# Fused attention and feed-forward kernel: the second set-aside score moved up by half a row, and full-height products between two score pairs

## The chip, the cores and the metric

The kernel runs on one core of one Trainium2 chip. Its time is the device time of one execution in microseconds (us), and what is compared is the median over several executions. TensorE multiplies matrices and writes its results to eight banks of accumulators (PSUM); VectorE (DVE), ScalarE (ACT) and GpSimd (POOL) do the rest of the arithmetic, and SyncE (SP) issues most of the transfers. The engines run side by side and wait for each other only through semaphores.

## The reference

All tensors are float32. `x` is 2048 x 512; attention has 32 heads of 16 channels, the feed-forward layer 1792 hidden units.

```python
xn = layernorm(x)
q, k, v = split_heads(xn @ wqkv)               # 32 heads of 16
p = softmax(einsum("bhqd,bhkd->bhqk", q, k) * 16 ** -0.5)
s = merge_heads(einsum("bhqk,bhkd->bhqd", p, v)) @ wo
h = relu(xn @ w1 + b1) ** 2
g = silu(h @ w2 + b2)
out = x + s * g
```

## The kernel before, in words

To keep precision, every large operand is held as two rounded halves, a high part and a low part, and a product is the sum of three: high by high, high by low, low by high.

After a first stage (normalising, transposing, queries, keys, values) comes the main loop, 128 turns of it. A turn handles four steps; one step is one block of 128 keys against 512 queries for four heads. For a step, four scores are computed, one for each head (`score`, L282). Each uses only 64 rows of the array (16 channels, four times over for the parts), so two run at the same time: one on the lower half of the rows (half 0), the other on the upper half (half 1). Such a pair of products I call a row of work. `scores(i, p)` makes a row, a score pair of 128 x 1024 in a buffer `S`, and `exps` (L286, ScalarE) turns it into exponentials straight from there. There are two buffers `S` in the main loop.

One step in four, the last of the turn, is set aside: `aside(i, p, hp)` writes one single score to the one bank `lin` (called `single`), and VectorE copies it to SBUF (L305); when two copies are there, ScalarE takes the exponential from SBUF. A set-aside score fills one half of a row, and there are four of them in a turn. As there is one bank, each must wait until the one before it has been copied.

Between these stands filler: the matrix products of the feed-forward layer and, in the last sixteen turns, of the output projection. They are written as pairs of `Block`s, two results of 128 x 512 in the two banks of `spare`. A block's list `todo` holds its products over 128 rows; `issue` (L330) does one of them on one half of the rows, so that a product needs two issues, one on each half, in any order. `lin(0, 1)` issues one product on each half: a row of filler. `lin(0)` or `lin(1)` alone fills the half beside a set-aside score. In the first part of a pair, half 0 works on block 0 and half 1 on block 1; `swap()` issues what is left and exchanges them; the second `swap()` calls the blocks' `evict`, in which VectorE reads `spare`.

Most pairs of blocks have twelve products each and take two turns, with the swap between the turns. The blocks of `second` with g = 0 have six products each. They start and end in one turn (`make and end` in the loop), with the first swap in the middle of it: the two-pair turns, eight of 128. Every full turn has six score pairs, four set-aside scores and 24 halves of filler: twenty rows. At its end `values` (L538) multiplies the exponentials by the values, 32 products of 128 rows and 32 columns of the array for four steps.

The order of instructions on each engine is the order of the program text; nothing reorders it. The waits follow from the data. The order of TensorE's rows before, in a turn that isn't a two-pair turn: score pair 1; set-aside 1 beside filler; score pair 2; four rows of filler; filler beside set-aside 2; score pair 3; two rows; score pair 4; set-aside 3 beside filler; two rows; score pair 5; two rows; filler beside set-aside 4; score pair 6; values. Score pairs 5 and 6 belong to the next turn's first step. In a two-pair turn before: five rows of filler ahead of set-aside 2; nothing between score pairs 3 and 4, where the swap is; then set-aside 3, one row, score pair 5, four rows, set-aside 4, score pair 6.

Of the kernel before, what the change touches and what calls it, by code (L numbers as in the profile page):

```python
# [73 lines left out]
def fast_path(tc, sb, ps, env):  # L74
# [6 lines left out]
    mm = nc.tensor.matmul  # L81
# [4 lines left out]
    def t(shape, dt, tag):  # L86

        cnt[0] += 1
        p = ps if tag in ("S", "lin", "acc") else sb
        if tag in BUFS:  # L90
            turn[tag] = turn.get(tag, -1) + 1
            n = turn[tag] % BUFS[tag]
            tag = f"{tag}{places[n] if tag == 'S' else n}"
        return p.tile(shape, dt, tag=tag, name=f"{tag}_{cnt[0]}")
# [181 lines left out]
    ptile = {}  # L276

    def score(i, p, hp, dst):
        qd, qc, kb = steps[i]
        k, q = ka[qd, kb // 8], qa[qd, qc]  # L280
        r = slice(64 * hp, 64 * hp + 64)
        mm(dst, k[r, p, 128 * (kb % 8):128 * (kb % 8) + 128], q[r, p], start=True, stop=True)  # L282

    def exps(i, p, src):
        if src is not None:
            act.activation(ptile[i, p], src, AF.Exp, scale=SCALE)  # L286

    def place(i, p):
        ptile[i, p] = t([128, 2, 512], FT, f"P{2 * ((i - 1) % 4) + p}")

    def scores(i, p):

        if i < len(steps):
            sc = t([128, 2, 512], FT, "S")
            place(i, p)
            for hp in range(2):
                score(i, p, hp, sc[:, hp])
            return sc

    def aside(i, p, hp):  # L300

        if hp == 0:
            place(i, p)
        score(i, p, hp, single)
        dve.tensor_copy(ptile[i, p][:, hp], single)  # L305
# [5 lines left out]
    class Block:  # L311


        def __init__(self, lhs, rhs, ks, evict, late=(), upper=()):

            pairs = [(a, b) for a, b in ((0, 0), (0, 1), (1, 0))]
            todo = ([(k, a, b) for a, b in pairs for k in ks if k not in late] +
                    [(k, a, b) for k in late for a, b in pairs])
            self.todo = todo, [d for d in todo if d[0] not in upper]
            self.lhs, self.rhs, self.evict, self.at = lhs, rhs, evict, [0, 0]  # L320

        def issue(self, half, bank):
# [8 lines left out]
               stop=n == len(self.todo[half]) - 1 and self.at[other] > 0)  # L331
            return True

    pair, swapped = [None], [0]

    def lin(*halves):
        if pair[0]:  # L340
            for half in halves:
                j = half ^ swapped[0]
                pair[0][j].issue(half, lin_banks[j])

    def swap():
        if pair[0]:
            while any([pair[0][half ^ swapped[0]].issue(half, lin_banks[half ^ swapped[0]]) for half in range(2)]):
                pass
            swapped[0] ^= 1
            if not swapped[0]:  # L350
                pair[0][0].evict()
                pair[0] = None
# [21 lines left out]
    def split_piece(eng=None):  # L374
        if at_piece[1] == len(pieces):
            return
        j, layer, m = pieces[at_piece[1]]
        at_piece[1] += 1
        raw, q = raws.pop(0), PAIRS[m][1]
        wf[layer, m] = [t([128, 4, 256] if layer == 1 else [128, 2, 512], FR, f"wf{layer}{p}{q}") for p in "hl"]  # L380
        split(*wf[layer, m], raw, eng or dve, pool)
        load_piece()
# [15 lines left out]
    def second(c, g, i):  # L398
        ms = [m for m in range(len(PAIRS)) if PAIRS[m][0] == g]
        h, w = [hid[m] for m in ms], [wf[2, m] for m in ms]  # L400

        def evict():
            if g == 0:
                y[c, i] = t([128, 2, 512], FT, f"y{i}")
            old = b2b.unsqueeze(1).broadcast_to([128, 2, 512]) if g == 0 else y[c, i]
            dve.tensor_tensor(y[c, i], spare, old, op=OP.add)
            if g == 3:
                complete.add((c, i))

        return [Block(lambda p, k, j=j: h[k // 2][p][:, k % 2, 128 * j:128 * j + 128],  # L410
                      lambda p, k: w[k // 2][p][:, k % 2], range(2 * len(ms)), evict)
                for j in (2 * i, 2 * i + 1)]
# [8 lines left out]
    for c in ORDER:  # L421
        for m, (g, _) in enumerate(PAIRS):
            fill += [(lambda m=m: first(m), False), (None, True)]
            if m in (1, 2, 4, 6):
                for i in range(2):
                    make = lambda c=c, g=g if m > 1 else 0, i=i: second(c, g, i)
# [9 lines left out]
    for i in range(4):  # L436
        part = vt[:, 4 * i:4 * i + 4]
# [11 lines left out]
    for n in (0, 0, 1, 1, 0, 1, 2):  # L449
# [15 lines left out]
    todo = [[(k, a, 0) for n in (0, 2) for a in range(2) for k in (n, n + 1)],  # L465
            [(k, a, 0) for a in range(2) for k in range(4)]]
# [65 lines left out]
    def values(i):  # L532
        qd, qc, kb = steps[i]
        if kb == 0:
            acc[0] = t([128, 512], FT, "acc")
        for j in (1, 2, 3, 0) if i % 2 else (0, 1, 2, 3):
            o = (4 * qd + j) * 17
            mm(acc[0][32 * j:32 * j + 32], vt[:, kb, o:o + 32], ptile[i, j // 2][:, j % 2],  # L538
               start=kb == 0, stop=kb == NK - 1)

    def finish(i):

        qd, qc, kb = steps[i]
        if kb < NK - 1:
            return
        if i == len(steps) - 1:
            return
        ou = t([128, 512], FT, "ou")
        cast(act if turn_ends_first[0] else dve, ou, acc[0])
        sp.dma_start(zdram[qd][qc], ou[16::32])  # L550
        for j in range(4):
            sp.dma_start(udram[qd // 2][qc][0, qd % 2, :, j], ou[32 * j:32 * j + 16])
        n = i // 4
        events.setdefault(2 * n + 2, []).insert(0, (load_sums, (qd, qc)))
        at(n + 2, rowsums, qd, qc)
# [174 lines left out]
    def happen(time):  # L730
        for fn, a in events.pop(int(2 * time), ()):
            fn(*a)


    n = turn["S"]
# [3 lines left out]
    lin_banks = [spare[:, 0], spare[:, 1]]  # L739
# [3 lines left out]
    def rest(i, dst):  # L743

        group(dst, lambda p: onorm[2, 3][p][:, cut[i]], lambda p: wos[0][p][:, 3])

    def end_rest(i, src):

        o = t([128, 512], FT, f"wf2{'hl'[i // 2]}{i % 2}")
        dve.scalar_tensor_tensor(o, src, 0.5, gsb[2, i // 2][:, i % 2], op0=OP.mult, op1=OP.mult)  # L750
        pool.dma_start(out[1024 + 128 * i:1152 + 128 * i], o, accum_op=OP.add)

    turn_ends_first = [False]
    for n in range(TURNS):
        i = 4 * n
        happen(n)
        make, end, split_now = fill[n]
        if make:
            pair[0] = make()
        exps(i + 1, 0, scores(i + 1, 0))  # L760
        aside(i + 3, 0, 0)
        lin(1)
        exps(i + 1, 1, scores(i + 1, 1))
        for _ in range(5 if make and end else 4):
            lin(0, 1)
        if make and end:
            lin(0)
            aside(i + 3, 0, 1)
            exps(i + 2, 0, scores(i + 2, 0))
            swap()  # L770
            exps(i + 2, 1, scores(i + 2, 1))
            aside(i + 3, 1, 0)
            lin(1)
            exps(i + 3, 0, ptile[i + 3, 0])
            lin(0, 1)
            last = [scores(i + 4, 0)]
            for _ in range(4):
                lin(0, 1)
        else:
            lin(0)  # L780
            aside(i + 3, 0, 1)
            exps(i + 2, 0, scores(i + 2, 0))
            lin(0, 1)
            lin(0, 1)
            exps(i + 2, 1, scores(i + 2, 1))
            aside(i + 3, 1, 0)
            lin(1)
            exps(i + 3, 0, ptile[i + 3, 0])
            lin(0, 1)
            lin(0, 1)  # L790
            last = [scores(i + 4, 0)]
            lin(0, 1)
            lin(0, 1)
        lin(0)
        aside(i + 3, 1, 1)
        exps(i + 3, 1, ptile[i + 3, 1])
        last.append(scores(i + 4, 1))
        for p in range(2):
            exps(i + 4, p, last[p])
        if n == TURNS - 1:  # L800
            two = t([128, 2, 512], FT, "S")
            rest(0, two[:, 0])
        turn_ends_first[0] = n < LAST and end and fill[n][0] is None and fill[n - 1][2] and n % per in (7, 15, 23)
        swap()
        if n == LAST - 1:
            gsb.update({(2, i): y[2, i] for i in range(2)})
        if n == TURNS - 1:
            end_rest(0, two[:, 0])
        happen(n + 0.5)
        if split_now:  # L810
            split_piece()
        for j in range(4):
            values(i + j)
        finish(i + 3)
# [5 lines left out]
    zc, r = t([128, 16], FT, "zc"), t([128, 16], FT, "rc")  # L820
# [3 lines left out]
    half = [slice(0, 256), slice(256, 512)]  # L824
# [11 lines left out]
    for i in range(4):  # L836
        for j in range(4):
            mm(small[32 * j:32 * j + 32, 0, cut[i]], r[:, 4 * i + j:4 * i + j + 1].broadcast_to([128, 32]), ident,
               start=True, stop=True)
# [19 lines left out]
    for j in range(2):  # L859
        for todo in ((0, 0), (0, 1)), ((1, 0),):  # L860
            for i in (2 * j, 2 * j + 1):
                group(lins[i], lambda p: (h, l)[p][:, cut[i]], lambda p: wlast[0][:, p],
                      start=len(todo) == 2, stop=len(todo) == 1, todo=todo)
# [120 lines left out]
```

## Time and profile before

| | |
|---|---|
| median of 3 runs | 1272.64 us (1272.08 to 1272.99) |
| profiled execution, its own time | 1271.87 us |
| span of that execution | 1270.1 us |
| granted TensorE clock, mean | 0.997 of full speed |
| main loop: from the first value product to that of the last turn | 154.8 to 1249.2 us |
| ordinary turn, from value products to value products | 8.555 us, median |
| two-pair turn | 9.14 to 9.16 us, eight of them |
| exponential from a buffer `S` (L286) | 1021 ns, 768 of them |
| exponential from SBUF (L286) | 1061 ns, 256 of them |
| copy of a set-aside score (L305) | 692 ns, 512 of them |

The page gives, for each engine, its busy time, share of the span and instruction count (PEld is TensorE's loading of weights, which goes on beside its products). The chain is followed back from the last instruction to what released each step. A line of the timeline reads: start, length, engine, line in the kernel, operation, result<-operands, shape, count of merged instructions, and in brackets the idle time before and what ended it. Matmul records overlap and their ends are modelled, so it is their starts that are compared; a product whose weights come late is recorded as starting with its load and as longer than the usual 0.39 us.

### The profile page before, as it was taken

Reading aid. Unit: us, or ns where it says so; the run is one execution under the profiler, and the core shown is the slowest. Engines: PE = TensorE matmul, PEld = TensorE weight load, DVE = VectorE, ACT = ScalarE, POOL = GpSimd, SP = SyncE. Lnnn points to the kernel's source line nnn. Section 1 sums busy time; section 2 is a strip of 40 time slices with the busy share of each in tenths; the row PEclk is TensorE's granted clock in tenths of the full one; section 3 lists DMA queues with packets and bytes.
Section 4 is the critical chain, followed back from the end, with each engine's and each line's share of the span. In section 5 each row is a group of like instructions: output and inputs, shape, how many; then the busy total and the mean of one; then the engine's idle time right before and its main releaser. Section 6 shows DMA issues by size and latency. Waiting matters only on the chain.

```text
span 1270.1 us, 24789 instructions
## 1 busy us (share of the span) xinstructions
PE 1257.2 (99%) x9925; PEld 720.9 (57%) x9925; DVE 678.0 (53%) x1064; ACT 1034.1 (81%) x1123; POOL 259.1 (20%) x150
## 2 busy tenths in 40 slices
PE   9999999999999999999999999999999999999997
PEld 7888755555555455555555555555555555545553
DVE  5542255455555554545465455555554545566655
ACT  4222588889899898898988889899889989998883
POOL 5000122122211221312022221220331212322112
PEclk9999999999999999999999999999999999999998
DMA  7565513132233232121423222333222122463445
GB/s 269 206 230 203 211 45 101 58 93 60 76 125 109 60 107 61 43 88 48 152 73 109 60 76 60 93 125 104 55 66 86 50 88 59 142 216 123 145 130 118
DMA packets 84940, 137.32 MB, mean 108 GB/s; under 512 B 26058, under 2 KB 40408, under 8 KB 83284
## 3 DMA queue, kind: packets, MB, share of 16 engines
q1 hardware_dynamic: 81668, 126.25, 30.4%
q0 software_dynamic: 2720, 8.65, 2.4%
q8 instruction: 79, 1.29, 0.4%
q10 hardware_dynamic: 432, 0.79, 0.2%
q14 instruction: 41, 0.34, 0.1%
HBM read 94.24 MB, written 41.41 MB: 107 GB/s over the span
## 4 chain that ended last, share of the span: by engine, by line
PE 96%; DVE 2%; ACT 1%; POOL 0%; DMA 0%; issue 0%; ACTq 0%; DVEq 0%
PE acc L538 36%; PE spare L330 26%; PE S L282 16%; PE S L111 9%; PE lin L282 7%; DVE P L305 1%; PE S L204 1%; POOL hl L104 0%; DMA P<-in_A_x_dram 0%; PE acc L111 0%; DVE st L166 0%; ACT P L286 0%; ACT wf2h L98 0%; PE spare L664 0%; DVE T L186 0%
## 5 line engine op out<-in xcount | busy, mean ns | idle before, releaser
L286 ACT ACTIVATE P<-S 128x1024 f32<-128x1024 f32 x768 | 732.5, 1021 | 67.8 <-PE S L282 64.4
L305 DVE COPY P<-lin 128x512 f32<-128x512 f32 x512 | 354.1, 692 | 467.6 <-PE lin L282 338.3
L538 PE MATMUL acc<-P,vt 128*32 128x512 f32 x4096 | 466.0, 595 | 0.0
L282 PE MATMUL S<-QA,KA 64*128 64x512 f32 x1536 | 332.6, 422 | 0.1
L286 ACT ACTIVATE P<-P 128x1024 f32<-128x1024 f32 x256 | 271.5, 1061 | 43.7 <-DVE P L305 43.5
L538 PEld LDWEIGHTS acc<-P,vt 128*32 128x32 f32 x4096 | 120.0, 109 | 272.9 <-issue 272.9
L282 PEld LDWEIGHTS S<-QA,KA 64*128 64x128 f32 x1536 | 145.0, 183 | 160.3 <-ACT P L286 142.9
L282 PE MATMUL lin<-QA,KA 64*128 64x512 f32 x512 | 213.0, 416 | 1.0 <-DVE P L305 0.5
L104 POOL TENSOR_TENSOR wf1l<-wr,wf1h 128x1024 fp32r<-128x1024 f32 x28 | 66.8, 2385 | 404.4 <-DVE wf1h L100 135.2
L330 PE MATMUL spare<-xl,wf1h 64*128 64x512 f32 x504 | 122.4, 400 | 0.0
L104 POOL TENSOR_TENSOR hl<-T,hh 128x1024 fp32r<-128x1024 f32 x28 | 67.6, 2416 | 242.2 <-DVE hh L100 139.6
L104 POOL TENSOR_TENSOR wf2l<-wr,wf2h 128x1024 fp32r<-128x1024 f32 x28 | 66.7, 2384 | 207.3 <-PE acc L538 139.0
L330 PE MATMUL spare<-wf2l,hh 64*128 64x512 f32 x448 | 106.8, 398 | 0.0
L282 PEld LDWEIGHTS lin<-QA,KA 64*128 64x128 f32 x512 | 94.1, 184 | 22.3 <-DVE P L305 14.0
L330 PE MATMUL spare<-xh,wf1l 64*128 64x512 f32 x504 | 96.1, 392 | 0.0
L330 PE MATMUL spare<-xh,wf1h 64*128 64x512 f32 x504 | 95.5, 390 | 0.0
L330 PE MATMUL spare<-wf2h,hh 64*128 64x512 f32 x448 | 87.6, 391 | 0.0
L330 PE MATMUL spare<-wf2h,hl 64*128 64x512 f32 x448 | 84.5, 390 | 0.0
L330 PEld LDWEIGHTS spare<-xl,wf1h 64*128 64x128 f32 x504 | 67.0, 184 | 8.4
L330 PEld LDWEIGHTS spare<-xh,wf1h 64*128 64x128 f32 x504 | 59.7, 184 | 9.9
L330 PEld LDWEIGHTS spare<-xh,wf1l 64*128 64x128 f32 x504 | 59.7, 185 | 8.6
L98 ACT CAST P<-S 128x512 fp32r<-128x512 f32 x30 | 17.6, 587 | 57.6 <-PE S L111 55.9
(202 smaller groups left out, 996.5 us busy)
## 6 DMA issues: line engine op xcount, KB each, us to landing
wr<-in_B_w_dram SPq DMA_DIRECT2D x56, 512.0 KB
KA<-kd SPq DMA_DIRECT2D x64, 256.0 KB
QA<-qd SPq DMA_DIRECT2D x128, 128.0 KB
kd<-P SPq DMA_DIRECT2D x15, 512.0 KB
qd<-P SPq DMA_DIRECT2D x15, 512.0 KB
u<-ud SPq DMA_DIRECT2D x15, 512.0 KB
P<-in_A_x_dram SPq DMA_DIRECT2D x8, 512.0 KB
xd<-KA SPq DMA_DIRECT2D x4, 1024.0 KB
```

The source lines that it names most:

```text
L98: act.copy(dst, src)
L104: leng.tensor_tensor(lo, src, hi.bitcast(FT), op=OP.subtract)
L111: mm(dst, lhs(a, k), rhs(b, k), start=n == 0, stop=n == len(todo) - 1)
L204: nc.tensor.transpose(pt[:, k, 128 * j:128 * j + 128], xnorm[c, i][:, j, 128 * k:128 * k + 128], ident)
L282: mm(dst, k[r, p, 128 * (kb % 8):128 * (kb % 8) + 128], q[r, p], start=True, stop=True)
L286: act.activation(ptile[i, p], src, AF.Exp, scale=SCALE)
L305: dve.tensor_copy(ptile[i, p][:, hp], single)
L330: mm(bank, self.lhs(a, k)[r], self.rhs(b, k)[r], start=n == 0 and self.at[other] == 0, stop=n == len(self.todo[half]) - 1 and self.at[othe ...
L538: mm(acc[0][32 * j:32 * j + 32], vt[:, kb, o:o + 32], ptile[i, j // 2][:, j % 2], start=kb == 0, stop=kb == NK - 1)
```

## The change

Two things change in the main loop, both in TensorE's order alone.

In an ordinary turn three rows of filler, and not four, stand ahead of the second set-aside score. Then the upper half's next filler product is cut in two by columns: its first 256 columns are issued before the set-aside score, its last 256 after it (`issue_part`). The lower half does a whole filler product beside each. So the set-aside score stands half a row earlier in the upper half's order, and that half has one product and one weight load more.

In a two-pair turn the set-aside score stands one whole row earlier. Each half issues five of the six products of its block, ahead of the swap and after it; the sixth product of each block (the last of the list, popped from it) is issued once on all 128 rows (`issue_whole`), both between score pairs 3 and 4. After that the order of the rest of the turn is that of all turns.

```diff
-            self.todo = todo, [d for d in todo if d[0] not in upper]
+            self.todo = todo[:], [d for d in todo if d[0] not in upper]
...
+        def issue_whole(self, bank):
+            n = len(self.todo[0]) - 1
+            k, a, b = self.todo[0].pop()
+            assert (k, a, b) == self.todo[1].pop() and n in self.at and 0 in self.at
+            mm(bank, self.lhs(a, k), self.rhs(b, k), start=False, stop=False)
+
+        def issue_part(self, half, bank, part):
+            n = self.at[half]
+            if n >= len(self.todo[half]):
+                return
+            assert 0 < n < len(self.todo[half]) - 1
+            k, a, b = self.todo[half][n]
+            r, c = slice(64 * half, 64 * half + 64), slice(256 * part, 256 * part + 256)
+            self.at[half] += part
+            mm(bank[:, c], self.lhs(a, k)[r], self.rhs(b, k)[r, c], start=False, stop=False)
...
+    def lin_part(half, part):
+        if pair[0]:
+            j = half ^ swapped[0]
+            pair[0][j].issue_part(half, lin_banks[j], part)
...
-        for _ in range(5 if make and end else 4):
+        for _ in range(3):
             lin(0, 1)
+        lin(0)
         if make and end:
+            lin(1)
             lin(0)
             aside(i + 3, 0, 1)
-            exps(i + 2, 0, scores(i + 2, 0))
+        else:
+            lin_part(1, 0)
+            aside(i + 3, 0, 1)
+            lin(0)
+            lin_part(1, 1)
+        exps(i + 2, 0, scores(i + 2, 0))
+        if make and end:
+            for j in range(2):
+                pair[0][j].issue_whole(lin_banks[j])
             swap()
-            exps(i + 2, 1, scores(i + 2, 1))
-            aside(i + 3, 1, 0)
-            lin(1)
-            exps(i + 3, 0, ptile[i + 3, 0])
-            lin(0, 1)
-            last = [scores(i + 4, 0)]
-            for _ in range(4):
-                lin(0, 1)
         else:
-            lin(0)
-            aside(i + 3, 0, 1)
-            exps(i + 2, 0, scores(i + 2, 0))
             lin(0, 1)
             lin(0, 1)
-            exps(i + 2, 1, scores(i + 2, 1))
-            ...
+        exps(i + 2, 1, scores(i + 2, 1))
+        aside(i + 3, 1, 0)
+        lin(1)
+        exps(i + 3, 0, ptile[i + 3, 0])
+        lin(0, 1)
+        lin(0, 1)
+        last = [scores(i + 4, 0)]
+        lin(0, 1)
+        lin(0, 1)
         lin(0)
         aside(i + 3, 1, 1)
```

More of the change, by code (lines that the diff above doesn't have):

```diff
@@ L763, in fast_path @@
         exps(i + 1, 1, scores(i + 1, 1))
-        for _ in range(5 if make and end else 4):
+        for _ in range(3):
             lin(0, 1)
+        lin(0)
         if make and end:
+            lin(1)
             lin(0)
             aside(i + 3, 0, 1)
-            exps(i + 2, 0, scores(i + 2, 0))
-            swap()
-            exps(i + 2, 1, scores(i + 2, 1))
-            aside(i + 3, 1, 0)
-            lin(1)
-            exps(i + 3, 0, ptile[i + 3, 0])
-            lin(0, 1)
-            last = [scores(i + 4, 0)]
-            for _ in range(4):
-                lin(0, 1)
-        else:
-            lin(0)
-            aside(i + 3, 0, 1)
-            exps(i + 2, 0, scores(i + 2, 0))
+        else:
[7 more added lines that the diff above has]
+                pair[0][j].issue_whole(lin_banks[j])
+            swap()
+        else:
             lin(0, 1)
             lin(0, 1)
-            exps(i + 2, 1, scores(i + 2, 1))
[L786 to L793, printed above, removed]
+        exps(i + 2, 1, scores(i + 2, 1))
[7 more added lines that the diff above has]
+        lin(0, 1)
         lin(0)
```

## The prediction

> **What bounds the kernel.** I read the page's busy shares and chain first, then who waited for whom, then turns line by line. Times in us.
>
> ```profile
> PE 1257.2 (99%) x9925; PEld 720.9 (57%) x9925; DVE 678.0 (53%) x1064; ACT 1034.1 (81%) x1123; POOL 259.1 (20%) x150
> PE 96%; DVE 2%; ACT 1%; POOL 0%; DMA 0%; issue 0%; ACTq 0%; DVEq 0%
> ```
>
> TensorE carries 96% of the chain, so only its order and holes count. From the starts of the value products (L538) an ordinary turn lasts 8.555 (median); each of the eight two-pair turns lasts 9.14 to 9.16, 0.60 more, with the same twenty rows of half-height products. Those turns have holes:
>
> ```profile
> 434.29 0.19 PEld L282 LDWEIGHTS S<-QA,KA 64*128 64x128 f32 x2 [0.84 <-ACT P L286]
> 434.40 0.19 PEld L282 LDWEIGHTS lin<-QA,KA 64*128 64x128 f32 x1
> ...
> 436.24 0.20 PEld L282 LDWEIGHTS S<-QA,KA 64*128 64x128 f32 x2
> 436.89 0.18 PEld L282 LDWEIGHTS S<-QA,KA 64*128 64x128 f32 x2 [0.45 <-ACT P L286]
> 437.44 0.18 PEld L282 LDWEIGHTS lin<-QA,KA 64*128 64x128 f32 x1 [0.37 <-DVE P L305]
> 437.44 0.29 PEld L330 LDWEIGHTS spare<-wf2h,hh 64*128 64x128 f32 x3
> 438.06 0.18 PEld L282 LDWEIGHTS S<-QA,KA 64*128 64x128 f32 x2 [0.32 <-ACT P L286]
> ```
>
> These are weight loads in one two-pair turn. The score pair at 436.89 waits for a score buffer (an exponential), the set-aside score at 437.44 for the copy out of the one bank `lin`, the score pair at 438.06 for a buffer again. Two readings serve throughout: rows follow each other every 0.23 (434.63, 434.87, 435.10, 435.33), and a late load lets its product begin 0.11 later (the load after 434.29 stands at 434.40). The same spots of an ordinary turn, loads, then products, then copies:
>
> ```profile
> 470.65 0.18 PEld L282 LDWEIGHTS lin<-QA,KA 64*128 64x128 f32 x1
> ...
> 471.67 0.19 PEld L282 LDWEIGHTS S<-QA,KA 64*128 64x128 f32 x2 [0.20 <-ACT P L286]
> 471.99 0.18 PEld L282 LDWEIGHTS lin<-QA,KA 64*128 64x128 f32 x1
> ...
> 472.61 0.19 PEld L282 LDWEIGHTS S<-QA,KA 64*128 64x128 f32 x2
> ```
>
> ```profile
> 470.57 0.60 PE L330 MATMUL spare<-wf2l,hh 64*128 64x512 f32 x2
> 470.81 0.39 PE L282 MATMUL lin<-QA,KA 64*128 64x512 f32 x1
> 471.02 0.42 PE L282 MATMUL S<-QA,KA 64*128 64x512 f32 x2
> ...
> 472.79 0.39 PE L282 MATMUL S<-QA,KA 64*128 64x512 f32 x2
> ...
> 473.48 0.39 PE L282 MATMUL lin<-QA,KA 64*128 64x512 f32 x1
> 473.49 0.39 PE L330 MATMUL spare<-wf2h,hl 64*128 64x512 f32 x1
> ```
>
> ```profile
> 469.91 0.69 DVE L305 COPY P<-lin 128x512 f32<-128x512 f32 x1 [1.89 <-PE lin L282]
> 471.25 0.69 DVE L305 COPY P<-lin 128x512 f32<-128x512 f32 x1 [0.65 <-PE lin L282]
> ```
>
> The second set-aside score may load only when the first copy is out (470.60, and its load stands at 470.65); it runs from 470.81, is copied from 471.25 to 471.94, and the third, loaded at 471.99, begins at 472.10. The score pair before it began at 471.77, so 472.00 was possible: a hole of 0.10.
>
> The last two fences give prices: what a change between full-height and half-height products costs, and how fast short products run.
>
> ```profile
> 144.79 0.64 PEld L111 LDWEIGHTS S<-xh,wf2l 128*128 128x128 f32 x3
> 145.78 0.30 PEld L282 LDWEIGHTS S<-QA,KA 64*128 64x128 f32 x4 [0.35 <-issue]
> 146.44 0.76 PEld L111 LDWEIGHTS acc<-xh,hh 128*128 128x128 f32 x4 [0.36 <-issue]
> ```
>
> ```profile
> 14.70 1.11 PE L204 MATMUL S<-ident,T 128*128 128x128 f32 x8 [0.47 <-DVE T L186]
> ```
>
> The last full product starts at 145.46, the half-height load follows 0.32 later and begins 0.11 after that: 0.43 where a row takes 0.23, so 0.20 per change. The way back (146.12 to 146.44) is the same. Short products of 128 columns, each with its own weights, run every 0.11.
>
> **Part 1: the two-pair turns (8).** Filler stays at twenty rows: two full products stand for four half ones. Removed: one row before the second set-aside score and two after the fourth score pair; added: two full products and two changes of height. On that turn's clock:
> - Set-aside two is in row 8 instead of 9. Row 8 is at 436.02 (before: 436.01), later than its bank's release (435.82 + 0.05 + 0.11), so no wait. Its copy ends at 436.02 + 0.44 + 0.69 = 437.15 (436.25 to 436.69 shows the 0.44).
> - Score pair three is row 9, 436.25; the full products begin at 436.25 + 0.43 = 436.68 and at 436.91; score pair four at 436.91 + 0.43 = 437.34 (now 437.00). Its buffer came free at 436.84: the 0.30 hole is filled with work.
> - Set-aside three at 437.57 (now 437.55), with no wait for the copy; two rows; score pair five at 438.26. Its exponential ended near 437.77: no hole.
> - Two rows; set-aside four at 438.95 (bank released at 437.57 + 0.49 + 0.69 + 0.05, ready 0.11 later, 438.91: cover of 0.04, and 0.01 lost for each 0.01 beyond it); score pair six at 439.18; values 0.33 later, 439.51. Now 439.86.
>
> So -0.35 each, **-2.8 in eight turns**. Bounds: a change of height at nothing would give -0.61 a turn (then the copy binds set-aside three, at 437.31), -4.9; at twice 0.20 it would give +0.05 a turn, +0.4. I take 0.20, measured in both directions on these very score products.
>
> **Part 2: the other turns (120).** One filler product of the upper half is cut in two parts of 256 columns, with the second set-aside score between them: one load and one product more each, about 120 in all; no column more.
> - The set-aside score's place in the order moves by half a row (0.115), but its bank is released as before: load 470.65, start 470.76 instead of 470.81. Gain 0.05. The lower half's next filler load now queues behind that waiting load (470.66, ready 470.77, wanted at 470.79): covered by 0.02 here, but where VectorE is late both halves wait.
> - The copy ends 0.05 earlier, set-aside three begins at 472.05; by the array alone score pair five would be at 472.74 instead of 472.79.
> - The price: the upper half idles from the end of part one (470.57 + 0.12 = 470.69) to 470.76, so part two runs at 470.99 and the upper score of pair three starts at 470.99 + 0.12 = 471.11 instead of 471.04. Its exponential, which began at 471.53 as soon as that score was there, begins at 471.60 and ends at 472.63 instead of 472.56. Score pair five needs that buffer: load at 472.68 instead of 472.61, start 472.79. As now. The 0.05 is given back.
>
> A part's 0.12 is my choice; no row shows 256 columns. Bounds: 0.11 (the 128-column row) and 0.23 (a full row). 0.12 is half a row, and 0.11 shows that short products with their own loads keep pace. Worked the same way through 118 ordinary turns, with each one's starts, the sum is -0.8 at 0.114, +0.1 at 0.122, +3.4 at 0.154 (about the median distance here from the second set-aside load to its product) and +14.7 at 0.23. I take **-0.3**.
>
> No DMA and no instruction of VectorE, ScalarE, GpSimd or SyncE is added or removed. **Sum: -3.1.** The profiled execution took 1271.87 (span 1270.1), so 1268.8; the median shown, 1272.64, is 0.77 above that execution, so **1269.5** (-0.25%).
>
> **Rivals.**
> - *A part costs a full row* (other side). If a part beside a 512-column product may not end before it, the set-aside score stays at 470.81 and the upper score of pair three comes 0.2 later, the exponential and score pair five with it: +0.12 a turn, +14.7 - 2.8: 1284.5. It decides from a part of about 0.175 on (+0.2%). Against it: at 473.48 the set-aside score starts 0.01 before the filler product that stands ahead of it in the order, so the halves do not go in lockstep.
>
>   The Trainium skill (TensorE: Matmul & The Clock Gate, Part 3, The mechanism) has a rule that gives this rival: "MATMULs are pc-monotone in start AND end". By that rule the time would be 1284.5; the two starts at 473.48 and 473.49 disagree with it by 0.01, with equal lengths only.
> - *A part costs 0.15*, because its load shows: +3.4 - 2.8, 1273.2, no change. For it: late set-aside loads here stand 0.13 to 0.15 ahead of their product; against: the half was still streaming then, and holes show 0.11.
> - *The ScalarE link does not bind*: the exponential is not delayed and the 0.05 stays: -5.9 - 2.8, 1263.9. Against: in more than 100 of 118 turns it starts 0.10 to 0.12 after its score's recorded end.
> - *The changes of height cost 0.40 each*: +0.4 - 0.3, 1272.7, no change.
>
> **How the numbers follow.** My forecast has 0.53 (its own range 1267.5 to 1271, so about a quarter of it is "same"), the full-row part 0.14, the 0.15 part 0.18, the free ScalarE link 0.10, the dear changes 0.05. 0.2% is 2.5, about what a measurement can tell from no change: faster means below 1270.1. Faster: 0.42 + 0.10, same: 0.11 + 0.13 + 0.04, slower: 0.14 + 0.06 from the edges of the middle cases. The range 1264 to 1277 leaves out the full-row part and small tails.
>
> **What the new profile would show.** Two-pair turns of about 8.80; no ACT or DVE wait of 0.3 in them, but two gaps of 0.35 before loads of the full products and of the score pair after. In ordinary turns the second set-aside load unmoved (1.58 after the first score), its product near 1.69, the exponential of the third pair near 2.53 instead of 2.46, the length within 0.03 of 8.555. Wrong if that exponential starts at 2.6 or later, if it doesn't move, or if a two-pair turn stays above 9.0.

## The result, and the profile after

The changed kernel takes 1267.18 us (median of 6 runs, 1266.77 to 1267.82) against 1272.57 us before: ratio 0.9959, 95% interval 0.9949 to 0.9969. That is 5.4 us less, where 3.1 were forecast. The profiled execution took 1266.77 us, its span was 1265.0.

TensorE still carries the chain. From the page, busy shares and then the chain by engine and by line:

```profile
PE 1252.7 (99%) x10029; PEld 715.2 (57%) x10029; DVE 677.8 (54%) x1064; ACT 1041.3 (82%) x1123; POOL 258.9 (20%) x150
PE 96%; DVE 2%; ACT 1%; issue 1%; POOL 1%; DMA 0%; DVEq 0%; ACTq 0%
```

The instruction count of PE rose by 104 (120 products cut in two add 120; in each of the eight two-pair turns two full products stand for four half ones, which takes 16 away), and the time fell. Measured between the first value product of the first turn and that of the last, the main loop went from 1094.4 to 1089.9 us. Of these 4.5 us, 2.8 lie in the eight two-pair turns (sum 73.24, now 70.42; median 9.158, now 8.803) and 1.7 in the other 119 (1021.15, now 1019.45; median 8.557, now 8.538; the prediction gives 8.555 for the same median).

The weight loads of one two-pair turn after the change (start, length, engine, line, operation, result<-operands, shape, count, idle before and what ended it):

```profile
424.22 0.19 PEld L282 LDWEIGHTS S<-QA,KA 64*128 64x128 f32 x2 [0.84 <-ACT P L286]
424.32 0.19 PEld L282 LDWEIGHTS lin<-QA,KA 64*128 64x128 f32 x1
...
425.93 0.19 PEld L282 LDWEIGHTS S<-QA,KA 64*128 64x128 f32 x2
426.48 0.30 PEld L339 LDWEIGHTS spare<-wf2h,hl 128*128 128x128 f32 x2 [0.36 <-issue]
427.15 0.19 PEld L282 LDWEIGHTS S<-QA,KA 64*128 64x128 f32 x2 [0.37 <-ACT P L286]
427.26 0.19 PEld L282 LDWEIGHTS lin<-QA,KA 64*128 64x128 f32 x1
...
427.95 0.19 PEld L282 LDWEIGHTS S<-QA,KA 64*128 64x128 f32 x2
```

The three waits of 0.45, 0.37 and 0.32 are gone. In their place stand two gaps, ahead of the full products (426.48) and of score pair four (427.15). The second is put down to ACT, but the buffer's release was not what ended it: the exponential that reads that buffer had ended at 426.76, and the gap is as long as the first, which waits for nothing; the last full product had started 0.32 before. Set-aside three and score pair five load with no gap (427.26, 427.95).

An ordinary turn after the change: the loads, then the products, then ScalarE's exponentials from `S` (merged, beginning with pair one's).

```profile
468.68 0.18 PEld L350 LDWEIGHTS spare<-wf2l,hh 64*128 64x128 f32 x1
468.99 0.18 PEld L282 LDWEIGHTS lin<-QA,KA 64*128 64x128 f32 x1
...
470.27 0.18 PEld L282 LDWEIGHTS lin<-QA,KA 64*128 64x128 f32 x1
...
471.02 0.19 PEld L282 LDWEIGHTS S<-QA,KA 64*128 64x128 f32 x2 [0.22 <-ACT P L286]
```

```profile
468.91 0.28 PE L350 MATMUL spare<-wf2l,hh 64*128 64x256 f32 x1
469.03 0.46 PE L282 MATMUL lin<-QA,KA 64*128 64x512 f32 x1
469.13 0.39 PE L330 MATMUL spare<-wf2l,hh 64*128 64x512 f32 x1
469.33 0.28 PE L350 MATMUL spare<-wf2l,hh 64*128 64x256 f32 x1
469.36 0.48 PE L282 MATMUL S<-QA,KA 64*128 64x512 f32 x2
```

```profile
468.01 3.87 ACT L286 ACTIVATE P<-S 128x1024 f32<-128x1024 f32 x4 [0.61 <-PE S L282]
```

The part starts at 468.91 and the set-aside score 0.12 later, but that score is 0.46 long instead of 0.39: its weights came late, at 468.99, when the bank was released, so it began 0.07 after its recorded start, at 469.10 (468.99 and the 0.11 of a late load). Part two follows at 469.33, and the merged score pair (469.36, 0.48 long) shows its upper score starting 0.09 after its lower one. The four exponentials take 3.87; in the same turn of the kernel before they took 3.80:

```profile
469.67 3.80 ACT L286 ACTIVATE P<-S 128x1024 f32<-128x1024 f32 x4 [0.60 <-PE S L282]
```

So the delay of the upper score is in ScalarE's chain. At the other end, score pair five now waits for its buffer (471.02, 0.22 idle), where it didn't before.

Medians over 118 ordinary turns (the 119 but for the last), from the traces, in us after the recorded start of the turn's first score. The forecast column is the turn that the prediction works out. In that turn score pair five stood at 3.72 before, too, so for it the forecast was no change:

| | before | after | forecast |
|---|---|---|---|
| load of set-aside two | 1.581 | 1.581 | 1.58 |
| set-aside two begins | 1.734 | 1.687 (load + 0.106) | 1.69 |
| upper score of pair three | 1.967 | 2.038 | 2.04 |
| its exponential | 2.459 | 2.528 | 2.53 |
| load of set-aside three | 2.930 | 2.862 | 2.87 |
| score pair five begins | 3.730 | 3.712 (load 3.606 + 0.106) | 3.72 |

### The profile page after: what moved, and what is told of

Same layout as the page of the kernel before. It is cut to its first block, busy times and chain, and to the rows that moved or that the text cites. A ratio compares the mean times of both kernels' runs of the same rounds, so it can differ in the third digit from the quotient of the medians.

```text
span 1265.0 us, 24997 instructions
## 1 busy us (share of the span) xinstructions
PE 1252.7 (99%) x10029; PEld 715.2 (57%) x10029; DVE 677.8 (54%) x1064; ACT 1041.3 (82%) x1123; POOL 258.9 (20%) x150
## 4 chain that ended last, share of the span: by engine, by line
PE 96%; DVE 2%; ACT 1%; issue 1%; POOL 1%; DMA 0%; DVEq 0%; ACTq 0%
PE acc L561 36%; PE spare L330 24%; PE S L282 17%; PE S L111 9%; PE lin L282 8%; PE spare L350 1%; PE S L204 1%; ACT P L286 0%; PE spare L339 0%; POOL hl L104 0%; DMA P<-in_A_x_dram 0%; DVE P L305 0%; PE acc L111 0%; DVE st L166 0%; ACT wf2h L98 0%
## 5 line engine op out<-in xcount | busy, mean ns | idle before, releaser
L282 PE MATMUL S<-QA,KA 64*128 64x512 f32 x1536 | 344.3, 423 | 0.3
L282 PEld LDWEIGHTS S<-QA,KA 64*128 64x128 f32 x1536 | 163.9, 183 | 177.0 <-ACT P L286 141.1
L330 PE MATMUL spare<-xl,wf1h 64*128 64x512 f32 x440 | 109.3, 392 | 0.0
L330 PE MATMUL spare<-wf2l,hh 64*128 64x512 f32 x400 | 96.9, 391 | 0.0
L330 PE MATMUL spare<-wf2h,hl 64*128 64x512 f32 x416 | 80.9, 391 | 0.0
L330 PEld LDWEIGHTS spare<-xl,wf1h 64*128 64x128 f32 x440 | 62.4, 184 | 0.7
```

What stands on the lines that cost most here:

```text
L330: mm(bank, self.lhs(a, k)[r], self.rhs(b, k)[r], start=n == 0 and self.at[other] == 0, stop=n == len(self.todo[half]) - 1 and self.at[othe ...
```

## The experiments

Each kernel was timed beside the kernel before; the edits are shown against the changed kernel unless said otherwise, inside the turn of the main loop.

**One part alone.** First the two-pair turns alone, the filler ahead of set-aside two as before:

```diff
-            lin_part(1, 0)
-            aside(i + 3, 0, 1)
-            lin(0)
-            lin_part(1, 1)
+            lin(1)
+            lin(0)
+            aside(i + 3, 0, 1)
```

> Only the two-pair turns are changed; ordinary turns stand as before. The account so far (two parts that add up): eight turns at 8.80 instead of 9.155 and the others at 8.557, so -2.8 us against the kernel before (ratio 0.9978). Rival, that the two parts need each other (the shorter two-pair turns only pay when the ordinary turns are also shorter): less than 1.5 us. The remaining 0.6 us of the measured gain, which lies outside the main loop, would show here too if the change causes it.

Measured: 1269.04 us, ratio 0.9972 (0.9960 to 0.9983), 3.65 less than before in medians. The profile: two-pair turns 8.804, ordinary turns 8.556, main loop 1091.7, so 2.7 us in the loop, all of it in the two-pair turns. The rival falls: that part pays alone what it pays in the whole.

Then the ordinary turns alone, the two-pair turns written out as before:

```diff
+        if make and end:
+            lin(1)
+            lin(0, 1)
+            lin(0)
+            aside(i + 3, 0, 1)
+            exps(i + 2, 0, scores(i + 2, 0))
+            swap()
+            exps(i + 2, 1, scores(i + 2, 1))
+            ...
+        else:
             lin_part(1, 0)
             aside(i + 3, 0, 1)
             lin(0)
             lin_part(1, 1)
```

> Only the ordinary turns are changed; two-pair turns stand as before. The account so far: a median of 8.538 instead of 8.557 in 119 turns, -1.7 us in their sum, at most -2.4 with the part outside the loop (ratio 0.998 to 0.999). Rival: nothing, as my forecast had it (-0.3 us).

Measured: 1269.92 us, ratio 0.9979 (0.9970 to 0.9988), 2.8 less. The profile: ordinary turns 8.539, two-pair turns 9.156, main loop 1092.8, so 1.5 us in the loop. My forecast of 0.3 for this part was too small, and its direction right.

The two loops add up: 2.7 + 1.5 = 4.2, against 4.5 for both. The medians don't add up as well (3.65 + 2.8 = 6.4, against 5.4), but each of these has an interval of 1.2 to 1.5 us to either side. What the single steps of the two-pair turns give (the earlier set-aside score, the full products, the new places of the rows around score pair five) was not tried apart.

**A whole row instead of half.** Set-aside two moved up by a whole row, nothing cut:

```diff
-            lin_part(1, 0)
             aside(i + 3, 0, 1)
             lin(0)
-            lin_part(1, 1)
+            lin(1)
```

> The second set-aside score moved up by a whole row in ordinary turns, filler uncut; two-pair turns as in the changed kernel. Theory 1 (the bank's release sets that score's start, and a late upper score of pair three is passed on by ScalarE): the score begins at 1.69 after the turn's first score, no earlier than with half a row, the upper half then does a whole filler product before pair three, whose upper score begins at 2.15 instead of 2.04; the exponential at 2.64, score pair five at 3.82 instead of 3.71: ordinary turns 8.65, +11 us on them, -2.8 from the two-pair turns, so +8 us against the kernel before (ratio 1.006 to 1.007). Theory 2 (only the start of the set-aside score and its copies count): the same start, so the same time as the changed kernel, or less, ratio 0.996.

Measured: 1279.20 us, ratio 1.0051 (1.0038 to 1.0065), slower than before by 6.5, where +8 was expected; the main loop in the profiles is longer by 7.7. Its ordinary turns last 8.650. The load of set-aside two stands at 1.582, where it stands before and after the change (1.581), so an earlier place in the order gives nothing beyond the bank's release. The upper score of pair three is at 2.153, its exponential at 2.639. Weight loads of one such turn:

```profile
472.34 0.18 PEld L282 LDWEIGHTS lin<-QA,KA 64*128 64x128 f32 x1
...
473.62 0.18 PEld L282 LDWEIGHTS lin<-QA,KA 64*128 64x128 f32 x1
...
474.47 0.18 PEld L282 LDWEIGHTS S<-QA,KA 64*128 64x128 f32 x2 [0.22 <-ACT P L286]
...
475.39 0.19 PEld L282 LDWEIGHTS S<-QA,KA 64*128 64x128 f32 x2 [0.16 <-ACT P L286]
```

The third set-aside score loads 1.28 after the second (1.35 before, 1.28 in the changed kernel), so VectorE's link is no longer than with the change; score pairs five and six both wait for ScalarE. This separates the theories: the same start of the set-aside score, and 12 us between the two kernels.

**The cut without the move.** Both parts ahead of set-aside two:

```diff
             lin_part(1, 0)
-            aside(i + 3, 0, 1)
-            lin(0)
             lin_part(1, 1)
+            lin(0)
+            aside(i + 3, 0, 1)
```

> The filler product is cut in two parts, but both stand ahead of the second set-aside score, which is where it was before; two-pair turns as in the changed kernel. If a part costs half a row (0.12): set-aside score at 1.74 as before, ordinary turns as before within 0.01, so the time of the kernel with the two-pair part alone, within 1.2 us (ratio 0.997 to 0.999). If the extra load and product cost by themselves, 0.03 to 0.11 per turn: +3 to +13 us on that.

Measured: 1268.88 us, ratio 0.9973 (0.9964 to 0.9983), within 0.2 us of the kernel with the two-pair part alone; both main loops are 1091.7. Its ordinary turns last 8.556, set-aside two is at 1.736. So 120 loads and 120 products more cost nothing that can be measured. In the changed kernel's trace the upper score of pair three starts 0.117 after part two (0.112 to 0.125 in 118 turns): a part costs half a row.

**Part two behind score pair three.** This leaves set-aside two where the change put it, and takes away only the delay of pair three's upper score:

```diff
             lin(0)
-            lin_part(1, 1)
         exps(i + 2, 0, scores(i + 2, 0))
+        if not (make and end):
+            lin_part(1, 1)
         if make and end:
```

> As the changed kernel, but in ordinary turns the second part of the cut filler product stands behind score pair three instead of ahead of it; the second set-aside score keeps its place. Theory 1 (the delay of pair three's upper score gives back most of what the earlier set-aside score gains, through ScalarE and the score buffer of pair five): upper score at 1.93 instead of 2.04, exponential at 2.45 instead of 2.53, pair five at 3.66 instead of 3.71 (set then by the copy and the array), ordinary turns 8.48 to 8.50 instead of 8.538: -5 to -6.5 us more than the changed kernel, 1261 to 1262 (ratio to before 0.991). Theory 2 (the gain is set by the set-aside score and its copies alone): no difference to the changed kernel, 1267.

Measured: 1262.58 us, ratio 0.9922 (0.9909 to 0.9936): 10.0 less than before in medians, nearly twice what the change gave. Ordinary turns last 8.494. The upper score of pair three is at 1.921; the lower one, at 1.957, is now the later of the two, and the exponential is at 2.455. The time is 0.6 above the 1261 to 1262 that theory 1 gave; theory 2, with 1267, falls. The same turn as above, products, loads and exponentials:

```profile
467.63 0.27 PE L350 MATMUL spare<-wf2l,hh 64*128 64x256 f32 x1
467.63 0.39 PE L330 MATMUL spare<-wf2h,hh 64*128 64x512 f32 x1
467.74 0.47 PE L282 MATMUL lin<-QA,KA 64*128 64x512 f32 x1
467.86 0.39 PE L330 MATMUL spare<-wf2l,hh 64*128 64x512 f32 x1
468.05 0.44 PE L282 MATMUL S<-QA,KA 64*128 64x512 f32 x2
468.28 0.27 PE L350 MATMUL spare<-wf2l,hh 64*128 64x256 f32 x1
```

```profile
468.99 0.18 PEld L282 LDWEIGHTS lin<-QA,KA 64*128 64x128 f32 x1
...
469.67 0.19 PEld L282 LDWEIGHTS S<-QA,KA 64*128 64x128 f32 x2 [0.15 <-ACT P L286]
469.80 0.42 PEld L330 LDWEIGHTS spare<-wf2h,hl 64*128 64x128 f32 x4
```

```profile
466.73 3.80 ACT L286 ACTIVATE P<-S 128x1024 f32<-128x1024 f32 x4 [0.60 <-PE S L282]
```

Part two now stands behind the score pair, the four exponentials are back at 3.80, and score pair five loads 0.68 after set-aside three, where the changed kernel has 0.75. Its products begin 0.128 after that load in the median turn (3.536 to 3.664), and not the 0.106 of a product that waits for its weights: the array sets their start and not the buffer. Set-aside two and its copies are where the change had them (1.618 and 2.116 in both, recorded). This shows that in the changed kernel the late upper score gave back 0.044 of the median turn through ScalarE.

**Score pair five one row later**, another way around the same wait:

```diff
+        for _ in range(3):
             lin(0, 1)
-        lin(0, 1)
         last = [scores(i + 4, 0)]
         lin(0, 1)
-        lin(0, 1)
```

> As the changed kernel, but score pair five stands one filler row later in all turns. Theory 1: pair five no longer meets its buffer's release, but pair six, which was 0.01 from its own (exponential of pair four ends at 4.47, start possible at 4.63, stands at 4.64), does: -0.01 a turn, -1.4 us against the changed kernel at most. If pair five's wait alone were what holds the turn, -0.05 a turn, -6 us.

Measured: 1265.37 us, ratio 0.9945 (0.9931 to 0.9958), 1.8 less than the changed kernel, a little more than the 1.4 that was expected at most; ordinary turns 8.521. The intervals of the two ratios overlap; the main loops in the profiles are 1088.0 here and 1089.9 there. The 6 us of the other reading did not come. The wait moved to pair six, whose load stands at 4.519, as in the changed kernel (4.521): ScalarE's chain, and not one pair's place, held the turn. And both together:

```diff
             lin(0)
-            lin_part(1, 1)
         exps(i + 2, 0, scores(i + 2, 0))
+        if not (make and end):
+            lin_part(1, 1)
...
+        for _ in range(3):
             lin(0, 1)
-        lin(0, 1)
         last = [scores(i + 4, 0)]
         lin(0, 1)
-        lin(0, 1)
```

> Part two behind score pair three, and score pair five one row later as well. If with part two behind pair three no score buffer binds any more, moving pair five changes nothing: 1262.6 within 0.6, ordinary turns 8.49. If ScalarE's link still binds there, about 1 to 2 us less, as moving pair five alone gave (8.521 instead of 8.538).

Measured: 1262.14 us, ratio 0.9925 (0.9908 to 0.9941), ordinary turns 8.491, within 0.5 us of part two's move alone: nothing that can be measured is left to gain from pair five once pair three is on time.

**Outside the main loop.** The medians fell further than the loops in the profiles, so both kernels were profiled again.

> The kernel before, profiled once more: is the 0.6 to 1 us by which the medians fall further than the main loop in the profiles (5.4 against 4.5, 3.65 against 2.7, 2.8 against 1.5) in the main loop or outside it? If outside: main loop again 1094.4 within 0.2, ahead of it and behind it together some 0.5 to 1 us more than in the first profile. If inside: a main loop of 1095 or more.

> The changed kernel, profiled once more, for the same question: main loop 1089.9 within 0.3, and the stretches ahead of and behind it as far from the first profile's (155.15 and 19.99) as chance takes them, some 0.5 us.

The kernel before: 1271.75 us, loop 1094.2. The changed one: 1266.79, loop 1089.9. Neither of the two answers I had laid out came: the loops repeat within 0.2, and what lies outside them is 175.7 and 175.8 in the two profiles of before, 175.1 and 175.2 in the two of the changed kernel. In the other seven profiles it is 175.1 to 175.8, though all kernels have the same instructions there. The medians of before were 1272.6, 1272.7, 1272.6 and 1271.7 in the four comparisons. So of the 5.4 us some 4.5 are in the loop and 0.9 are not: 0.6 lie outside the loop in the profiles, and 0.3 is how much nearer the changed kernel's profiled execution is to its median (the two profiled executions differ by 5.1). The profiles of kernels with the same instructions outside the loop spread by as much as those 0.6, so whether the change causes them stays open.

## Why the prediction was right, and where its size was off

- *Two-pair turns, -0.35 each, -2.8*: measured -0.355 and -2.81, and alone -2.8 in those turns. The steps hold one by one. In the turn that the prediction works out, score pair four begins 3.03 after the first score (3.05 forecast), score pair five 3.96 (3.97) and the values 5.21 (5.22). In the turn shown above, the full products load 0.55 after score pair three (a row and 0.32), and score pair four loads 0.67 after that (0.11 of a late load, a row, and 0.32 again). A change of height costs the 0.20 that the score products ahead of the main loop showed, and the rival with 0.40 is out.
- *The bank's release sets set-aside two*: its load did not move at all, 1.581 in both. The gain in its start was 0.047, not the half row of 0.115. The whole-row experiment shows it again.
- *A part costs 0.12*: 0.117. The rivals by which it costs 0.15 or a full row are out. Set-aside two runs from 469.10, 0.19 before the recorded end of the 512-column filler issued ahead of it (468.897 + 0.390), and part one's recorded end (469.19) is 0.10 before that filler's. Ends are modelled, so the starts say more: with part two behind pair three, the upper score of that pair starts at 468.053, 0.04 ahead of the lower one (468.097), which is issued first. The rule of the Trainium skill that stands beside the full-row rival (TensorE: Matmul & The Clock Gate, Part 3, The mechanism), by which matmuls start and end in program order, does not hold across the two halves here.
- *ScalarE gives it back*: right in mechanism (exponential at 2.528, 2.53 forecast; score pair five now waiting for its buffer), and shown by taking it away.
- *The term that was mis-sized* is the sum over the 118 ordinary turns, "-0.8 at 0.114, +0.1 at 0.122", taken as -0.3. Measured: -1.5 alone, -1.7 in the whole (0.07 of it in the last turn, which is not among the 118). By the prediction's own two figures a part of 0.117 gives about -0.5, so the price of a part explains 0.2 of what is missing. Score pair five begins 0.018 earlier in the median turn, and what I took is 0.003 a turn. With a link on each side of nearly equal length, 0.01 in a turn is 1.2 us in the kernel, and rows read to 0.01 can't give that; in which step the rest lies is not shown. A single turn can't show it either: the one that I worked out, at 469.07, went from 8.533 to 8.538 in the first two profiles and from 8.545 to 8.520 in the second two.
- The remaining 0.9 us of the measured difference had no term in the sum and has no cause found. With it, 1267.18 lies in the stated range, 1264 to 1277, but 0.3 below the 1267.5 to 1271 that the forecast gave for its own case; without it, the time would be inside both.

That two half-height rows could fill the hole of the two-pair turns without any change of height was not tried. My reason was that the two halves would follow each other into the same bank with nothing between them to order their sums; no run here tests that.

## What to carry to other kernels

Moving work earlier helps only as far as the resource that it waits for is free; look at the load's start in the trace before choosing how far to move it. When one chain (here VectorE's copies) is shortened, see what the filler that was put in its way now delays: of the places tried here, the best for the second part was behind the score pair that ScalarE was waiting for, and it nearly doubled the gain. Filler at the array's full height can close a hole that is longer than the two changes of height around it, 0.20 each here; in the two-pair turns that left 0.355 a turn.

## What the runs showed of the hardware

Products on the two halves of the array's rows keep no order among themselves: a 256-column product beside a 512-column one lets its half go on after 0.117, and a score issued second starts 0.04 ahead of the one issued first. Instructions are issued in the order of the program text, as the kernel's description says, but across the halves that is not the order of starts. The extra loads and products of the parts cost nothing that shows: 120 of each changed the median by less than 0.2 us and left the main loop at 1091.7. Going from half-height to full-height products and back showed the same 0.32 from the last start to the next load in both directions (426.161 to 426.482, 426.823 to 427.148), with two products between.
